# Seven quarter products for eight in the first channel product of blocks 1 to 3, and the second mixing layer in the order wr, wk, wv

## Chip, cores and metric

The kernel runs on one core of a Trainium2 chip. The metric is the device time of one execution in microseconds (us); of several executions the median is taken.

## What is computed

Three layers follow each other (reference, cut):

```python
x = attention(q, k, v, n_global, n_local)      # 2 x 8 heads x 768 x 64, joined to (2, 768, 512)
u = x + ((x.transpose(0, 2, 1) @ U) @ V).transpose(0, 2, 1)
x = u + np.maximum(u @ w_ch1, 0.0) @ w_ch2     # first channel layer: 512 -> 2048 -> 512
xk = mu_k * x + (1.0 - mu_k) * x_prev          # x_prev: x one token earlier, per batch
xr = mu_r * x + (1.0 - mu_r) * x_prev
k = np.maximum(xk @ w_k, 0.0)                  # 512 -> 1024
out = sigmoid(xr @ w_r) * (k * k @ w_v)        # 512 -> 512 and 1024 -> 512
```

Everything is float32. `x` has 1536 rows (2 batches of 768 tokens).

## The kernel before

The data lie with channels on the partitions (`yp`, four groups of 128 channels). The 1536 tokens are three chunks of 512: chunk 0 lies in the first batch, chunk 1 spans both (so its reads and writes of `yp` come in two pieces of 256), chunk 2 lies in the second. The first channel layer cuts its 2048 hidden channels into four blocks `g` of 512; block `g` needs the tiles `w1s` (its columns of `w_ch1`) and `w2s` (its rows of `w_ch2`).

Each matrix product is made of three passes (`PASS`): every operand is split into a high part and the remainder (low), and high*high, high*low and low*high are summed in PSUM. A product of 128 x 512 results over a depth of 512 is so 4 x 3 = 12 matmuls of 512 columns.

`m_ch1(g, c, f)` (L904) makes hidden tile `f` of block `g` and chunk `c`: 12 matmuls (L893) into a PSUM bank of tag `a`, ScalarE takes the relu as high part (L897), VectorE the low part (L901). `m_ch2(g, c, o)` (L909) makes 12 matmuls (L915) into a bank of tag `t` and VectorE adds them to `yp` (L919). There are four banks of each tag, so a matmul group waits until the group four before it on its tag has been read.

Weights arrive as 64-bit floats in pieces of 128 x 512 (512 KB), through three staging tiles `stg`. `bg` takes the next piece from the list `bgq`: VectorE and ScalarE turn it to float32 (`cvt` L655, L660, L664, L668), ScalarE writes the high part (L672), GpSimd the low part (L676). A staging tile is free for the next transfer when L668 has read it. Two slots each of the pools `sb`, `sc`, `sd` and three of `sa` hold weights, activations (`us`, the split input of a chunk; `rs`, a split hidden tile) and the mixed inputs.

`weave` interleaves lists of steps. The program on TensorE keeps the written order; on the other engines a scheduler orders the instructions at build time, so VectorE and ScalarE run each instruction in the order it set. The written order alternates first and second products:

```python
weave(st_ch1(1, 1, slot_b) + st_ch2(1, 0), st_bg(4))
weave(st_ch1(1, 2, slot_c) + st_ch2(1, 1), st_bg(4))
weave(st_ch1(2, 0, slot_b) + st_ch2(1, 2))
```

The second layer mixes each chunk with its shifted copy (`m_mix`, L1053 on GpSimd, L1055 on VectorE, split by L1057 and L1058), and then, per chunk, makes `k` (`m_k`: 96 matmuls L1071 in 8 tiles; relu, square and split by L1075 to L1081) and per tile of 128 tokens (`m_out`) the gate (12 matmuls L1090, sigmoid L1094) and the value (24 matmuls L1101), multiplied (L1104) and sent out (L1105).

## Time and profile before

| | |
|---|---|
| times of three runs | 518.87, 519.10, 520.76 us; median 519.1 |
| profiled execution | 521.29 us, of it a span of 519.4 us on the engines |
| TensorE matmuls | 504.9 us busy, 97% of the span |
| weight loads | 412.1 us, 79% |
| VectorE | 304.7 us, 59% |
| ScalarE | 217.7 us, 42% |
| GpSimd | 184.1 us, 35% |
| mean granted TensorE clock | 0.995 |

A matmul's busy time overlaps the next one's; the distance between two starts is the time it costs. Times in the rows count from the start of the span. Attention, the low-rank product and block 0 of chunk 0 fill the first 107 us; the rest is dense matmuls.

### The profile page before, as it was taken

The page shows a single profiled execution, that of the slowest core. Times are in us where ns is not written, and L with a number is a line of the kernel's source. Part 1 is how long each engine was busy: PE and PEld are TensorE (multiplying, and loading weights), DVE is VectorE, ACT ScalarE, POOL GpSimd, SP SyncE. Part 2 cuts the span into 40 slices and gives each one's busy share as a digit, 9 for nine tenths or more (in the row PEclk, how much of TensorE's full clock was granted, in tenths as well). Part 3 has the DMA queues.
Part 4 walks back from the last instruction along what each step waited for, and adds up shares of the span by engine and source line. Part 5 has one row for each costly group of instructions (what it writes and reads, how often), then busy time and mean ns, then how long its engine had stood idle before and what let it go on. Part 6 is the DMA issues. An engine that isn't in the chain of part 4 may idle for free.

```text
span 519.4 us, 8649 instructions
## 1 busy us (share of the span) xinstructions
PE 504.9 (97%) x3314; PEld 412.1 (79%) x3314; DVE 304.7 (59%) x672; ACT 217.7 (42%) x508; POOL 184.1 (35%) x247
## 2 busy tenths in 40 slices
PE   8899999989999999999999999999999999999995
PEld 4677688778888888888888888887888888888885
DVE  7899978989982826528265837796043522252110
ACT  6999986455521313214133312444912441144100
POOL 7767784034410404004040403636712442144100
PEclk9999999989999999999999999999999999999999
DMA  8988543313550311304113310031001000100001
GB/s 327 329 286 294 202 137 122 107 65 122 162 187 16 122 40 48 115 0 122 40 25 138 124 39 1 24 138 42 0 21 40 22 0 21 40 21 1 21 21 47
DMA packets 13586, 47.18 MB, mean 91 GB/s; under 512 B 1760, under 2 KB 2144, under 8 KB 13536
## 3 DMA queue, kind: packets, MB, share of 16 engines
...
## 4 chain that ended last, share of the span: by engine, by line
PE 81%; DVE 11%; DMA 2%; ACT 2%; issue 1%; POOL 1%; POOLq 0%; SPq 0%; DVEq 0%; ACTq 0%
PE aps L893 26%; PE bps L915 19%; PE pvs L1101 13%; PE kps L1071 11%; PE prs L1090 6%; DVE P L471 3%; PE tp L498 2%; DVE cvc L664 2%; DVE cvc L668 2%; PE s L463 2%; DMA stg<-in_w_dram 1%; PE warm L379 1%; DMA stg<-in_wv_dram 1%; DVE yp L919 1%; PE xa L513 1%
## 5 line engine op out<-in xcount | busy, mean ns | idle before, releaser
L893 PE MATMUL aps<-us,w1s 128*128 128x512 f32 x576 | 135.3, 393 | 0.0
L915 PE MATMUL bps<-rs,w2s 128*128 128x512 f32 x576 | 132.5, 389 | 0.0
L893 PEld LDWEIGHTS aps<-us,w1s 128*128 128x128 f32 x576 | 108.7, 189 | 22.7
L915 PEld LDWEIGHTS bps<-rs,w2s 128*128 128x128 f32 x576 | 108.0, 188 | 23.3 <-PE gps L792 0.8
L897 ACT ACTIVATE rs<-aps 128x512 fp32r<-128x512 f32 x48 | 28.4, 597 | 95.0 <-PE aps L893 94.7
L1071 PE MATMUL kps<-mix,wk 128*128 128x512 f32 x288 | 66.1, 389 | 0.4 <-ACT kf L1075 0.4
L1071 PEld LDWEIGHTS kps<-mix,wk 128*128 128x128 f32 x288 | 54.0, 188 | 12.0 <-ACT kf L1075 0.8
L1101 PE MATMUL pvs<-wv,kh 128*128 128x512 f32 (+1 forms) x208 | 61.9, 373 | 0.0
L901 DVE SCALAR_TENSOR_TENSOR rs<-aps,rs 128x512 fp32r<-128x512 f32 x48 | 32.7, 686 | 41.0 <-ACT rs L897 41.0
L664 DVE SCALAR_TENSOR_TENSOR cvc<-cvc,cvt 128x512 uint32<-128x512 uint32 (+1 forms) x53 | 48.6, 918 | 7.9 <-ACT cvc L660 6.4
L660 ACT ACTIVATE cvc<-stg 128x512 f32<-128x512 f32 (+1 forms) x53 | 35.2, 674 | 41.3 <-DMA stg<-in_w_dram 15.6
L919 DVE TENSOR_TENSOR yp<-bps,yp 128x512 f32<-128x512 f32 (+1 forms) x64 | 33.9, 550 | 25.5 <-PE bps L915 25.4
L491 POOL TENSOR_SCALAR P<-P,sm 128x192 f32<-128x192 f32 x96 | 42.1, 461 | 16.5 <-DVE sm L485 9.6
L1053 POOL TENSOR_SCALAR mixt<-yp,mu 128x512 f32<-128x512 f32 (+1 forms) x32 | 21.6, 682 | 74.1 <-DVE mixf L1055 29.6
L668 DVE SCALAR_TENSOR_TENSOR cvc<-stg,cvc 128x512 uint32<-128x512 uint32 x52 | 45.6, 885 | 0.7
L676 POOL TENSOR_TENSOR w2s<-cvc,w2s 128x512 fp32r<-128x512 f32 x16 | 23.2, 1467 | 63.5 <-ACT w2s L672 63.5
L1101 PEld LDWEIGHTS pvs<-wv,kh 128*128 128x128 f32 x208 | 38.1, 188 | 6.9
L676 POOL TENSOR_TENSOR w1s<-cvc,w1s 128x512 fp32r<-128x512 f32 x16 | 23.9, 1514 | 55.4 <-ACT w1s L672 54.8
L479 ACT ACTIVATE P<-P,nm 128x192 f32<-128x192 f32 x96 | 42.5, 447 | 1.5 <-DVE nm L471 1.4
L1081 POOL TENSOR_TENSOR kl<-kf,kh 128x512 fp32r<-128x512 f32 x24 | 31.0, 1293 | 30.6 <-ACT kh L1080 30.6
L1101 PE MATMUL pvs<-wv,kl 128*128 128x512 f32 (+1 forms) x104 | 38.8, 373 | 0.0
L1055 DVE SCALAR_TENSOR_TENSOR mixf<-yp,mu,mixt 128x512 f32<-128x512 f32 (+1 forms) x32 | 20.3, 653 | 29.8 <-POOL mixt L1053 29.7
...
## 6 DMA issues: line engine op xcount, KB each, us to landing
stg<-in_w_dram SPq DMA_DIRECT2D x32, 512.0 KB, 4.1
...
stg<-in_wk_dram SPq DMA_DIRECT2D x8, 512.0 KB, 4.2
stg<-in_wv_dram SPq DMA_DIRECT2D x8, 512.0 KB, 4.0
...
stg<-in_wr_dram SPq DMA_DIRECT2D x4, 512.0 KB, 3.6
```

The source lines that it names most:

```text
L479: nc.scalar.activation(out=Px, in_=Px, func=ACTF.Exp, scale=-1.0, bias=z["nm"][:, i, x:x + 1], accum_out=z["sm"][:, i, x:x + 1])
L491: engine.tensor_scalar(out=Px, in0=Px, scalar1=z["sm"][:, i, x:x + 1], scalar2=1.0, op0=ALU.mult, op1=ALU.mult)
L660: nc.scalar.activation(out=z["c"].bitcast(F32), in_=parts(z)[1].bitcast(F32), func=ACTF.Copy, scale=2.0 ** -112)
L664: nc.vector.scalar_tensor_tensor(out=z["c"], in0=z["c"], scalar=3, in1=z["t"], op0=ALU.logical_shift_left, op1=ALU.bitwise_or)
L668: nc.vector.scalar_tensor_tensor(out=z["c"] if plain is None else plain, in0=parts(z)[1], scalar=0x80000000, in1=z["c"], op0=ALU.bitwise_a ...
L676: engine.tensor_tensor(out=lo, in0=z["c"].bitcast(F32), in1=hi.bitcast(F32), op=ALU.subtract)
L893: nc.tensor.matmul(rs[g, c, f], lhsT=wsl(("w1", g), lw, kk, f * 128, 128), rhs=us[c][:, lx, kk, :], start=(kk == 0 and n == 0), stop=(kk = ...
L901: nc.vector.scalar_tensor_tensor(out=r[:, 1, f, :], in0=rs[g, c, f], scalar=0.0, in1=r[:, 0, f, :].bitcast(F32), op0=ALU.max, op1=ALU.subt ...
L915: nc.tensor.matmul(ps, lhsT=wsl(("w2", g), lw, f, o * 128, 128), rhs=r[:, lx, f, :], start=(n == 0), stop=(n == 11))
L919: nc.vector.tensor_tensor(out=ys, in0=ps[:, a:e], in1=ys, op=ALU.add)
L1071: nc.tensor.matmul(ps, lhsT=wsl("wk", lw, kk, f * 128, 128), rhs=xk[:, lx, kk, :], start=(n == 0), stop=(n == 11))
L1101: nc.tensor.matmul(pv, lhsT=ks[c][lx][:, f, t * 128:(t + 1) * 128], rhs=wsl("wv", lw, f, c0, c1 - c0), start=(n == 0), stop=(n == 23))
```

## The change

For blocks 1 to 3 the first products of chunks 1 and 2 are taken together (`st_pair`). With the block's weights A (hidden x input channels) and the inputs B (input channels x the two chunks) each cut into 2 x 2 quarters, the four quarters of A B need eight quarter products, each of 256 hidden channels, a depth of 256 and 512 tokens; Winograd's form needs seven:

- S1 = A21 + A22, S2 = S1 - A11, S3 = A11 - A21, S4 = A12 - S2, made by VectorE from the converted weights (tiles `raw`) and split into `w1x`;
- T1 = B12 - B11, T2 = B22 - T1, T3 = B22 - B12, and B21 - T2, made once, during block 0, by VectorE from `yp` and split into `diff` and, for T3, over a part of `us` of chunk 2 that is no longer needed after block 0;
- the products A11 B11, A12 B21, S4 B22, A22 (B21 - T2), S1 T1, S2 T2, S3 T3, six matmuls each for one of two tiles of hidden channels, added up by VectorE in tiles `sums` (seven additions L1023 and one ScalarE copy a tile), then relu (L1026) and low part (L1027) from there.

The order of the work becomes, for a block: the pair, then the first product of chunk 0, then the second products of chunks 2, 1 and 0; for block 3, which has no next block to load, chunks 0, 1 and 2. In the second layer the gates of a chunk (`m_r`) come ahead of its `m_k`, its weights are converted in the order wr, wk, wv; `sg` has six tiles of its own, VectorE makes every second low part of these weights, and the shifted product of `m_mix` moves from GpSimd to ScalarE.

```diff
+                        def add(_, z=z):
+                            a, b = z[0], z[1]
...
+                            nc.vector.tensor_tensor(out=s1, in0=a[:, 256:], in1=b[:, 256:], op=ALU.add)
+                            nc.vector.tensor_tensor(out=s3, in0=a[:, :256], in1=a[:, 256:], op=ALU.subtract)
+                            nc.vector.tensor_tensor(out=s2, in0=s1, in1=a[:, :256], op=ALU.subtract)
+                            nc.vector.tensor_tensor(out=s4, in0=b[:, :256], in1=s2, op=ALU.subtract)
...
+                            for i, t in enumerate(z["t"]):
...
+                                nc.scalar.copy(out=h, in_=t)
+                                nc.gpsimd.tensor_tensor(out=o, in0=t, in1=h.bitcast(F32), op=ALU.subtract)
...
+                    return [first, lambda: sub(t2, lo, t1), fourth, lambda: sub(z, lo, up)]
...
+                    def mm(n, j):
+                        a, b = OP[n]
+                        t = ps[n, j] = bank("at"[n in (1, 2, 3)], "pps")
+                        for k in range(2):
+                            for m, (lw, lx) in enumerate(PASS):
+                                nc.tensor.matmul(t, lhsT=a(lw, k, j), rhs=b(lx, k), start=(k == 0 and m == 0),
+                                                 stop=(k == 1 and m == 2))
...
+                        return [p1, p6, p2, p5, p3, p7, p4]
+
+                    return unit(0) + unit(1)
...
-                        nc.gpsimd.tensor_scalar(out=t[:, a:e], in0=yq, scalar1=mu[:, 2 + which, kk:kk + 1], scalar2=1.0,
-                                                op0=ALU.mult, op1=ALU.mult)
+                        nc.scalar.activation(out=t[:, a:e], in_=yq, func=ACTF.Copy, scale=mu[:, 2 + which, kk:kk + 1])
...
+                for g in range(1, NG):
+                    if g >= G0:
+                        weave(st_pair(g), st_bg(2))
...
+                    if g + 1 < NG:
+                        weave(st_ch1(g, 0, slot_b), st_bg(2))
+                        queue_pair(g + 1)
+                        weave(st_ch2(g, 2) + st_ch2(g, 1), st_bg(4))
+                        queue_g(g + 1, None, slot_c)
+                        weave(st_ch2(g, 0))
                 queue_weight("wr", wr, 4, 512, [slot_a("wr")])
...
+                queue_weight("wk", wk, 4, DK, [slot_d("wk0"), slot_d("wk1")])
+                weave(st_ch1(3, 0, slot_b), st_bg(4))
...
+                queue_weight("wv", wv, 8, 512, [slot_a("wv0"), slot_a("wv1")])
+                weave(st_ch2(3, 0), st_bg(3))
+                weave(st_ch2(3, 1), st_bg(2), st_mix(0, 1, slot_b))
+                weave(st_ch2(3, 2), st_bg(2), st_mix(0, 0, slot_b))
                 for c in range(NCH):
+                    weave([lambda t=t: m_r(c, t) for t in range(4)], st_bg(4))
```

**Place 1, TensorE, a block of the first layer.** `aps`, `pps` and `bps` are the PSUM banks of a first product, a quarter product and a second product; L915 is L948 and L893 is L926 in the changed kernel. Before:

```order
L893 MATMUL aps<-us,w1s 128x512 x48
L915 MATMUL bps<-rs,w2s 128x512 x48
L893 MATMUL aps<-us,w1s 128x512 x48
L915 MATMUL bps<-rs,w2s 128x512 x48
L893 MATMUL aps<-us,w1s 128x512 x48
L915 MATMUL bps<-rs,w2s 128x512 x48
L893 MATMUL aps<-us,w1s 128x512 x48
L915 MATMUL bps<-rs,w2s 128x512 x48
```

After, from the second half of block 1's pair on:

```order
L1019 MATMUL pps<-us,w1s 128x512 x6
L1019 MATMUL pps<-diff,w1x 128x512 x6
L1019 MATMUL pps<-us,w1s 128x512 x6
L1019 MATMUL pps<-diff,w1x 128x512 x6
L1019 MATMUL pps<-us,w1x 128x512 x12
L1019 MATMUL pps<-diff,w1s 128x512 x6
L926 MATMUL aps<-us,w1s 128x512 x48
L948 MATMUL bps<-rs,w2s 128x512 x144
L1019 MATMUL pps<-us,w1s 128x512 x6
```

Where groups of 48 alternated, the pair's groups of 6 (14 of them, 84 matmuls) stand ahead of chunk 0's 48, and all three second products (144) follow in one run.

**Place 2, VectorE, around the first hidden tiles of block 1 (before: those of chunk 0, after: those of the pair).** `cvt` is the first step of a weight conversion and waits for the transfer into its `stg`; `rs` is a low part; `sums` the additions of a pair. Before:

```order
L655 TENSOR_SCALAR cvt_2856<-stg_2854 128x512
L668 SCALAR_TENSOR_TENSOR cvc_2698<-stg_2694,cvc_2698 128x512
L901 SCALAR_TENSOR_TENSOR rs_2262<-aps_2263,rs_2262 128x512
L655 TENSOR_SCALAR cvt_2896<-stg_2894 128x512
L901 SCALAR_TENSOR_TENSOR rs_2262<-aps_2278,rs_2262 128x512
L901 SCALAR_TENSOR_TENSOR rs_2262<-aps_2303,rs_2262 128x512
L901 SCALAR_TENSOR_TENSOR rs_2262<-aps_2318,rs_2262 128x512
L919 TENSOR_TENSOR yp_63<-bps_2333,yp_63 128x512
L919 TENSOR_TENSOR yp_63<-bps_2347,yp_63 128x512
L919 TENSOR_TENSOR yp_63<-bps_2371,yp_63 128x512
```

After:

```order
L655 TENSOR_SCALAR cvt_2731<-stg_2729 128x512
L655 TENSOR_SCALAR cvt_2860<-stg_2858 128x512
L664 SCALAR_TENSOR_TENSOR cvc_2733<-cvc_2733,cvt_2731 128x512
L952 TENSOR_TENSOR yp_63<-bps_2338,yp_63 128x512
L668 SCALAR_TENSOR_TENSOR cvc_2733<-stg_2729,cvc_2733 128x512
L655 TENSOR_SCALAR cvt_2935<-stg_2933 128x512
L1023 TENSOR_TENSOR sums_2354<-pps_2363,sums_2354 128x512
L1023 TENSOR_TENSOR sums_2354<-pps_2371,sums_2354 128x512
L1023 TENSOR_TENSOR sums_2354<-pps_2381,sums_2354 128x512
L1027 SCALAR_TENSOR_TENSOR rs_2352<-sums_2354,rs_2352 128x512
L1023 TENSOR_TENSOR sums_2354<-pps_2399,sums_2354 128x512
L1023 TENSOR_TENSOR sums_2354<-pps_2409,sums_2354 128x512
```

The additions of the pair stand behind the last of the conversions of block 2's `w1s` and behind `cvt_2860` and `cvt_2935`, which wait for transfers.

**Place 3, VectorE, the first product of chunk 0 in block 3.** Its four low parts are `rs_3156` before and `rs_3446` after; `wk0` is a low part of wk. Before:

```order
L919 TENSOR_TENSOR yp_63<-bps_3141,yp_63 128x256 x2
L655 TENSOR_SCALAR cvt_3668<-stg_3666 128x512
L901 SCALAR_TENSOR_TENSOR rs_3156<-aps_3157,rs_3156 128x512
L901 SCALAR_TENSOR_TENSOR rs_3156<-aps_3172,rs_3156 128x512
L901 SCALAR_TENSOR_TENSOR rs_3156<-aps_3187,rs_3156 128x512
L901 SCALAR_TENSOR_TENSOR rs_3156<-aps_3202,rs_3156 128x512
L919 TENSOR_TENSOR yp_63<-bps_3217,yp_63 128x512
L664 SCALAR_TENSOR_TENSOR cvc_3639<-cvc_3639,cvt_3637 128x512
```

After, from behind the first of the four:

```order
L668 SCALAR_TENSOR_TENSOR cvc_3620<-stg_3616,cvc_3620 128x512
L934 SCALAR_TENSOR_TENSOR rs_3446<-aps_3472,rs_3446 128x512
L668 SCALAR_TENSOR_TENSOR cvc_3666<-stg_3662,cvc_3666 128x512
L655 TENSOR_SCALAR cvt_3716<-stg_3714 128x512
L664 SCALAR_TENSOR_TENSOR cvc_3718<-cvc_3718,cvt_3716 128x512
L676 TENSOR_TENSOR wk0_3444<-cvc_3666,wk0_3444 128x512
L934 SCALAR_TENSOR_TENSOR rs_3446<-aps_3497,rs_3446 128x512
L668 SCALAR_TENSOR_TENSOR cvc_3718<-stg_3714,cvc_3718 128x512
L655 TENSOR_SCALAR cvt_3768<-stg_3766 128x512
L664 SCALAR_TENSOR_TENSOR cvc_3770<-cvc_3770,cvt_3768 128x512
L655 TENSOR_SCALAR cvt_3818<-stg_3816 128x512
L934 SCALAR_TENSOR_TENSOR rs_3446<-aps_3522,rs_3446 128x512
```

The four low parts stood next to each other, and are now apart, with conversions of wk between them; two of these (`cvt_3768`, `cvt_3818`) wait for transfers ahead of the last low part.

## Rows read from the trace of the kernel before

**Rows 1.** page, parts 1 and 4: busy time by engine; the last chain by engine
```profile
PE 504.9 (97%) x3314; PEld 412.1 (79%) x3314; DVE 304.7 (59%) x672; ACT 217.7 (42%) x508; POOL 184.1 (35%) x247
...
PE 81%; DVE 11%; DMA 2%; ACT 2%; issue 1%; POOL 1%; POOLq 0%; SPq 0%; DVEq 0%; ACTq 0%
```

**Rows 2.** timeline, PE, blocks and second layer (start us, length us, then engine, line)
```profile
142.43 11.04 PE L893 MATMUL aps<-us,w1s 128*128 128x512 f32 x48
...
316.51 11.04 PE L893 MATMUL aps<-us,w1s 128*128 128x512 f32 x48
327.39 21.92 PE L915 MATMUL bps<-rs,w2s 128*128 128x512 f32 x96
349.15 11.04 PE L1071 MATMUL kps<-mix,wk 128*128 128x512 f32 x48
360.60 11.18 PE L1071 MATMUL kps<-mix,wk 128*128 128x512 f32 x48 [0.41 <-ACT kf L1075]
```

**Rows 3.** timeline, all engines, before the first matmuls of chunk 1
```profile
104.84 0.52 PE L823 MATMUL hps<-uv 96*128 96x256 f32 x3
105.60 0.43 DVE L655 TENSOR_SCALAR cvt<-stg 128x512 uint32<-128x512 uint32 x1 [1.60 <-DMA stg<-in_w_dram]
105.94 0.68 DVE L919 TENSOR_TENSOR yp<-bps,yp 128x512 f32<-128x512 f32 x1
...
106.68 1.16 PE L823 MATMUL hps<-uv 96*128 96x256 f32 x3 [1.32 <-DVE yp L919]
```

**Rows 4.** windows: busy us (count) of PE, PEld, DVE, ACT, POOL; clock; DMA
```profile
107.70:153.30 45.60, 45.60 (x195) 37.54 (x194) 41.75 (x64) 22.86 (x42) 18.51 (x12) 0.96 0.40 128
153.30:196.80 43.50, 43.50 (x193) 36.04 (x192) 21.30 (x33) 9.22 (x16) 5.96 (x4) 1.00 0.20 61
```

**Rows 5.** chain of waits, second layer (start us, us, engine, tile, line)
```profile
371.79 2.72 PE prs L1090 x12
374.51 5.44 PE pvs L1101 x24
```

**Rows 6.** groups by line and form: busy us, mean ns of one, idle before
```profile
L664 DVE SCALAR_TENSOR_TENSOR cvc<-cvc,cvt 128x512 uint32<-128x512 uint32 x52 | 47.9, 922 | 7.9 <-ACT cvc L660 6.4 <-DVE cvt L655 0.5
L668 DVE SCALAR_TENSOR_TENSOR cvc<-stg,cvc 128x512 uint32<-128x512 uint32 x52 | 45.6, 885 | 0.7
...
L901 DVE SCALAR_TENSOR_TENSOR rs<-aps,rs 128x512 fp32r<-128x512 f32 x48 | 32.7, 686 | 41.0 <-ACT rs L897 41.0
L1081 POOL TENSOR_TENSOR kl<-kf,kh 128x512 fp32r<-128x512 f32 x24 | 31.0, 1293 | 30.6 <-ACT kh L1080 30.6
...
L655 DVE TENSOR_SCALAR cvt<-stg 128x512 uint32<-128x512 uint32 x52 | 26.3, 507 | 8.5 <-DMA stg<-in_w_dram 4.5 <-DMA stg<-in_wk_dram 2.9 <-DMA stg<-in_wv_dram 0.8
...
L919 DVE TENSOR_TENSOR yp<-bps,yp 128x512 f32<-128x512 f32 x32 | 22.0, 686 | 21.3 <-PE bps L915 21.2
...
L1080 ACT CAST kh<-kf 128x512 fp32r<-128x512 f32 x24 | 14.9, 621 | 12.9 <-DVE kf L1079 12.6
...
L919 DVE TENSOR_TENSOR yp<-bps,yp 128x256 f32<-128x256 f32 x32 | 11.9, 414 | 4.2 <-PE bps L915 4.2
```

**Rows 7.** windows, PE: stretch, length, busy us (count), granted clock, DMA
```profile
13.00:19.00 6.00, 4.67 (x88) 1.00 0.97 322
108.00:112.00 4.00, 4.00 (x12) 0.57 0.00 0
```

**Rows 8.** timeline, PE, early attention
```profile
14.88 0.55 PE L498 MATMUL tp<-ident,P 128*128 128x128 f32 x3 [1.33 <-POOL P L491]
```

**Rows 9.** DMA issues: transfers of one weight piece, KB each, us to landing
```profile
stg<-in_wk_dram SPq DMA_DIRECT2D x8, 512.0 KB, 4.2
```

**Rows 10.** timeline, DVE, conversions of wk, beside POOL (next group) and alone
```profile
289.99 2.38 DVE L668 SCALAR_TENSOR_TENSOR cvc<-stg,cvc 128x512 uint32<-128x512 uint32 x2
...
294.13 0.69 DVE L668 SCALAR_TENSOR_TENSOR cvc<-stg,cvc 128x512 uint32<-128x512 uint32 x1
```

**Rows 11.** timeline, POOL, the same stretch
```profile
285.26 5.96 POOL L676 TENSOR_TENSOR wk<-cvc,wk 128x512 fp32r<-128x512 f32 x4 [15.77 <-ACT wk L672]
```

More of the change, by code (lines that the diff above doesn't have):

```diff
@@ L700, in queue_weight @@
                     wt[name] = (view, per)
-                    for kk in range(kt):
-                        for c0 in range(0, n, 512):
+                    for c0 in range(0, n, 512):
+                        for kk in range(kt):
                             hi = view[kk // per][:, 0, kk % per, c0:c0 + 512]
@@ L705, in queue_weight @@
                             s = src[kk * 128:(kk + 1) * 128, c0:c0 + 512]
-                            bgq.append((lambda d, s=s: nc.sync.dma_start(out=d, in_=s),
-                                        conv_steps((128, 512), hi, lo)))
+                            steps = conv_steps((128, 512), hi, lo)
+                            if name in ("wr", "wk", "wv") and kk % 2:
+                                steps[-1] = ("lo", lambda z, f=steps[-1][1]: f(z, "DVE"))
+                            bgq.append((lambda d, s=s: nc.sync.dma_start(out=d, in_=s), steps))
                 def wsl(name, l, kk, c0, n):
@@ L919, in m_ch2, with raw_tiles, diff_tiles @@
                         nc.vector.tensor_tensor(out=ys, in0=ps[:, a:e], in1=ys, op=ALU.add)
+                diffs, sums = [], {}
+                def raw_tiles():
+                    t = slots["sb"].tile([128, 4096], F32, tag="sb", name="sums")
+                    return [t[:, x * 512:(x + 1) * 512] for x in range(8)]
+                def diff_tiles():
+                    raws[:] = raw_tiles()
+                    diffs[:] = [diff_p.tile([128, 6144], F32R, name="diff").rearrange("p (l t k n) -> p l t k n", l=2, t=3, k=2)]
@@ new lines, in diff_raw, with sub, first, fourth @@
+                def diff_raw(k):
+                    d = diffs[0]
+                    (_, _, up), (_, _, lo) = chunk(yp, k, 2)[0], chunk(yp, k + 2, 2)[0]
+                    t1, t2, z, t4 = raws[4 * k:4 * k + 4]
+                    def sub(o, p, q):
+                        nc.vector.tensor_tensor(out=o, in0=p, in1=q, op=ALU.subtract)
+                    def first():
+                        for a, e, ys in chunk(yp, k, 1):
+                            sub(t1[:, a:e], up[:, a:e], ys)
+                    def fourth():
+                        for a, e, ys in chunk(yp, k + 2, 1):
+                            sub(t4[:, a:e], ys, t2[:, a:e])
+                    return [first, lambda: sub(t2, lo, t1), fourth, lambda: sub(z, lo, up)]
@@ new lines, in diff_split, with parts, diff_late @@
+                def diff_split(k):
+                    return [lambda x=x, t=t: parts(diffs[0], x, k, raws[4 * k + t]) for x, t in enumerate((0, 1, 3))]
+                raws = []
+                def parts(d, x, k, raw):
+                    h, o = d[:, 0, x, k, :], d[:, 1, x, k, :]
+                    nc.scalar.copy(out=h, in_=raw)
+                    nc.vector.tensor_tensor(out=o, in0=raw, in1=h.bitcast(F32), op=ALU.subtract)
+                def diff_late(k):
+                    h, o = us[2][:, 0, k, :], us[2][:, 1, k, :]
+                    nc.scalar.copy(out=h, in_=raws[4 * k + 2])
+                    nc.vector.tensor_tensor(out=o, in0=raws[4 * k + 2], in1=h.bitcast(F32), op=ALU.subtract)
@@ L1081, in m_k, with m_r @@
                     nc.gpsimd.tensor_tensor(out=kl[:, f, :], in0=kf, in1=kh[:, f, :].bitcast(F32), op=ALU.subtract)
[L1083 to L1084 removed]
+                gate = {}
+                def m_r(c, t):
                     xr = xs[c, 1]
@@ L1092, in m_out @@
                             n += 1
-                    sg = tmp_p.tile([128, 512], F32, tag="tmp", name="sg")
-                    nc.scalar.activation(out=sg, in_=pr, func=ACTF.Sigmoid)
+                    gate[c, t] = tmp_p.tile([128, 512], F32, tag="sg", name="sg", bufs=6)
+                    nc.scalar.activation(out=gate[c, t], in_=pr, func=ACTF.Sigmoid)
+                def m_out(c, t):
+                    b, i = divmod(c * 4 + t, NT)
+                    sg = gate[c, t]
                     last = (c, t) == (NCH - 1, 3)
```

112 lines of the change are left out of this document (88 added, 24 removed).

## The prediction

> **What bounds the kernel.** I read the page first: TensorE is busy for 97% of the span and makes 81% of the chain that ended last [rows 1]. Then the timeline of TensorE: from 142.43 to 316.51 sixteen groups of 48 matmuls follow each other, no row of them with an idle time in brackets. That is 174.08 / 16 = 10.88 us a group and 10.88 / 48 = 0.2267 us a matmul; 96 of L915 take twice that, 349.15 - 327.39 = 21.76 [rows 2]. After 107 us the time is therefore a count of matmuls times 0.2267, plus two idle times: 1.32 us at 106.68 [rows 3] and 0.41 at 360.60 [rows 2]. The next thing to look at is who could become late. VectorE is busy for 41.75 of the 45.6 us before block 1's second products end, and for only 21.30 of the 43.5 after them [rows 4]: the place of danger is where blocks 0 and 1 meet.
>
> **The change part by part.** The sum is made against the profiled execution, 521.29 us, and carried over to the median of the runs, 519.1, which lies 2.2 lower.
>
> *Matmuls.* A block's two chunks take 7 x 2 x 6 = 84 matmuls instead of 96 (place 1). Three blocks: 36 x 0.2267 = **-8.16**. A group of 6 opens a bank twice as often as one of 12. The chain has a group of 12 at 2.72 us and one of 24 at 5.44, both 0.2267 a matmul [rows 5], so a new bank costs nothing there; three groups of one matmul of 256 columns take 0.52 [rows 3], at most 0.06 each over half of 0.2267. The 54 more groups cost 0 to 3.2, and I take 0, by the nearer rows.
>
> *The idle time at 360.60* comes from ScalarE, which is late with k's relu because it still converts wv [rows 2]. In the change 48 gate matmuls, 10.88 us, stand ahead of the first k tile. **-0.41**; bounds -0.41 and 0.
>
> *The idle time at 106.68.* TensorE waits for VectorE's addition, and that stood behind a `cvt` which had waited 1.60 us for its transfer [rows 3]. In the changed order this `cvt` comes later; four half-width sums of weights stand ahead instead. The addition, at 105.94 before, comes at 105.94 - 1.60 - 0.4 + 4 x 0.41 = 105.6 by the half-width row [rows 6], 105.3 at half of the full width's 0.69. I take **-0.5**; bounds -1.3 (no wait) and +0.3.
>
> *The clock behind it.* In 108 to 112 TensorE is busy throughout at a granted 0.57, so most of it at the lower level, 1.2 GHz: 4 x 0.43 = 1.7 us lost [rows 7]. But an idle time of 1.33 us at 14.88 [rows 8] was followed by a clock of 1.00 [rows 7]. The trace does not tell which the shorter gap gets; I take 0, bounds -1.7 (no fall) and +1.7 (one more, behind a new gap). [...]
>
> *Additions of the pairs, VectorE.* Until the first of them, 12 full-width and 16 half-width differences and sums are added, 12 x 0.69 + 16 x 0.41 = 14.8 us, and four conversions move behind it, 4 x (0.92 + 0.89 + 0.51) = 9.3 [rows 6]. VectorE's 41.75 become 47.3 in 45.6 us [rows 4]: some 2 us late, and `cvt_2935` (place 2) can wait for a transfer. I put the first addition at 158, where its product ends at 153.3 + 2 x 1.36 = 156.0. TensorE does not wait for it: the bank is wanted again four groups of tag `a` later, at 153.3 + 8 x 1.36 = 164.2. In a pair VectorE has 11 instructions of 0.69, 7.5 us, for every 7 x 1.36 = 9.5 of TensorE, so it catches up; in blocks 2 and 3 it has 25 additions and low parts (17.3), 8 conversions (18.5), 8 half sums (3.3) and the additions to `yp` (8.8), 48 of 62.6 us. **0**; the upper bound is the first rival.
>
> *Chunk 0 of block 3* is the one place where a first product is followed by its own second product. The high part of its last tile is wanted 9 matmuls, 2.04 us, after that tile ends, the low part after 10, 2.27. In place 3 the last low part stands behind `cvt_3818`, whose transfer can only start when the second L668 has read its staging tile. The pair's last relu and low part hold the first two low parts and these L668 back to about 3.0 us before the tile ends; the transfer takes 4.2 [rows 9], landing at +1.2; behind it ScalarE makes a first step, a high part and the relu, 3 x 0.62 [rows 6], and VectorE the low part, 0.69: +3.0 or so against 2.27. **+0.8**; bounds 0 and 2.5 (0.8 with a fall of the clock behind it).
>
> *Between k and v* no gate lies any more. Of the last k tile relu, square, high and low part take 3 x 0.62 + 1.29 = 3.2 us [rows 6]; they are wanted 21 matmuls, 4.76, later. 0, with 1.6 to spare; two mixing steps on ScalarE in front, 4 x 0.62 = 2.5, would leave 0.9 a chunk, bound +2.7. The rest has cover: mixing steps on ScalarE lie beside at least 10.9 us of matmuls a chunk, `w1x` is split 22 us ahead of its use, and the last product, its multiplication and its transfer out are the same.
>
> Sum: -8.16 - 0.41 - 0.5 + 0.8 = -8.3. The profiled 521.29 becomes 513.0, the median **510.8**. The one case that this describes runs from 508.3 (no new wait, no fall of the clock) to 514.2 (a wait of 2.5 and a fall more).
>
> **Rivals.** *GpSimd holds VectorE up.* Two L668 took 2.38 us while GpSimd worked without a pause and 0.69 each alone [rows 10, 11], 0.5 more each. The added differences have both inputs in SBUF too, and lie among the same 12 GpSimd instructions, 18.5 us [rows 4]. I have counted about 7 of these as lost to VectorE in both kernels; if the other 11 are lost as well, the first addition comes at 169 and TensorE waits 5 us at 164.2: 515.8. For it speaks the full VectorE there; against it, that many additions read PSUM and L901 keeps its 0.69 [rows 6]. The Trainium skill, SBUF — State Buffer, in Who interferes with whom, says that an instruction with two SBUF inputs and one of GpSimd that reads SBUF shut each other out for a whole instruction; by that the sum would be 515.8, by the rows, where VectorE loses half of the time, 510.8.
>
> *A transfer decides block 3.* If one more transfer has to land ahead of the last low part, the wait at chunk 0's second product grows by 4.2 and the clock falls behind it, 1.7: 516.7, within half a per cent of before. For it: two `cvt` stand there. Against: three staging tiles, so both transfers run at once.
>
> *TensorE stops between quarter products: slower.* If VectorE is over 6 x 1.36 = 8.2 us late in the pairs, each product waits for a bank. One gap like that at 106.68 with the clock's fall costs 1.32 + 1.7 = 3.0; from four of them, 12, the gain of 8.3 is gone and the time is 522.8. It would need 8 us of lateness in blocks 2 and 3, where VectorE has 14 to spare. The Trainium skill, TensorE: Matmul & The Clock Gate, in the second failure mode, tells of a kernel whose cycling through PSUM banks left short idle times and a clock that swung; here groups of 12 ran at a clock of 1.00 [rows 4].
>
> That the change does not take out the matmuls can't be: the order shows 84.
>
> **How the numbers follow.** What a measurement of this kernel tells from no change is about 0.5%, 2.6 us. The forecast's case has 0.79; GpSimd 0.09 (515.8, still faster by 0.6%); the transfer 0.07 (same); stops between products 0.05 (slower). So faster 0.87, with one in a hundred of the first two falling short, same 0.08, slower 0.05. The range takes in the forecast's own, 508.3 to 514.2, and reaches to the GpSimd rival, 515.8; it leaves 0.12 out.
>
> **What would show it.** Right: in blocks 1 to 3 TensorE's rows of L1019 come in groups of 6 with 1.36 between their starts and no idle time, a block takes 62.6 us; no wait of L1221 on ScalarE; a wait of under 2 us ahead of the first L948 of block 3; the clock at 1.00 behind block 0. Wrong: idle times of L1019 released by VectorE L1023 (first or third rival), a wait of 4 us or more at block 3's L948 (second), a clock below 1.00 in a pair, a matmul pace above 0.2267 in groups of 6, or waits of L1256 on GpSimd's low part.

## Result and profile after

| | before | after |
|---|---|---|
| median of four runs each, same chip | 519.16 us (518.87 to 520.76) | 512.95 us (512.60 to 515.65) |
| ratio of the times | | 0.9885, 95% interval 0.9846 to 0.9925 |
| profiled execution, its span | 521.29, 519.4 us | 512.60, 510.8 us |
| mean granted TensorE clock | 0.995 | 0.997 |

The forecast was 510.8 us, in a range of 508.3 to 515.8: the time lies in the range and the sign is as forecast; the gain is 6.2 us instead of 8.3. The page of the changed kernel, as in [rows 1]: busy time of TensorE, its weight loads, VectorE, ScalarE and GpSimd, and the last chain by engine.

```profile
PE 496.1 (97%) x3278; PEld 404.0 (79%) x3278; DVE 357.5 (70%) x768; ACT 249.9 (49%) x566; POOL 167.9 (33%) x217
...
PE 84%; DVE 10%; DMA 2%; issue 1%; ACT 1%; POOL 1%; POOLq 0%; SPq 0%; DVEq 0%
```

VectorE has risen from 304.7 to 357.5 us and TensorE fallen from 504.9 to 496.1; TensorE still makes the chain. Its timeline from the end of block 0 on, in the columns of [rows 2]:

```profile
105.12 0.52 PE L856 MATMUL hps<-uv 96*128 96x256 f32 x3
106.28 1.16 PE L856 MATMUL hps<-uv 96*128 96x256 f32 x3 [0.65 <-DVE yp L952]
107.28 0.39 PE L926 MATMUL aps<-us,w1s 128*128 128x512 f32 x1
...
129.55 21.92 PE L948 MATMUL bps<-rs,w2s 128*128 128x512 f32 x96
151.31 1.52 PE L1019 MATMUL pps<-us,w1s 128*128 128x512 f32 x6
152.67 1.52 PE L1019 MATMUL pps<-diff,w1x 128*128 128x512 f32 x6
...
170.35 11.04 PE L926 MATMUL aps<-us,w1s 128*128 128x512 f32 x48
...
213.87 1.52 PE L1019 MATMUL pps<-us,w1s 128*128 128x512 f32 x6
...
306.35 2.20 PE L948 MATMUL bps<-rs,w2s 128*128 128x512 f32 x9
309.20 0.50 PE L948 MATMUL bps<-rs,w2s 128*128 128x512 f32 x1 [0.64 <-ACT rs L930]
311.20 30.71 PE L948 MATMUL bps<-rs,w2s 128*128 128x512 f32 x134 [1.50 <-DVE rs L934]
341.75 11.04 PE L1241 MATMUL prs<-wr,mix 128*128 128x512 f32 x48
352.62 21.92 PE L1221 MATMUL kps<-mix,wk 128*128 128x512 f32 x96
```

The second row answers to [rows 3]: 1.32 us of idle time have become 0.65. The pair of block 1 begins at 151.31, each group of six starts 1.36 after the one before, and the pair ends at 170.35, 19.04 later: 84 matmuls of 0.2267. From pair to pair lie 62.56 us. Nothing is in brackets until 309.20: there TensorE waits 0.64 for ScalarE's relu (L930) and at 311.20 another 1.50 for VectorE's low part (L934), at the second product of chunk 0 in block 3. Idle times are counted between modelled ends; by the distance between starts, 306.35 to 341.75 is 35.40 us for 144 matmuls, which make 32.64 at 0.2267 each, so that the two waits cost 2.76 and not 2.14. Behind them, gates and k tiles follow each other without a wait; the 0.41 of [rows 2] is gone.

The same 98 matmuls at the end of block 0 stand between these two rows of the kernel before, and between 107.28 and 129.55 after:

```profile
107.68 0.40 PE L893 MATMUL aps<-us,w1s 128*128 128x512 f32 x1
...
131.55 11.04 PE L915 MATMUL bps<-rs,w2s 128*128 128x512 f32 x48
```

That is 23.87 us against 22.27: the fall of the clock of [rows 7], which is missing after, cost 1.60. So by the starts in the two profiled executions: -8.16 for the matmuls, -0.57 at 360.60 (the second 48 began 11.45 behind the first instead of 10.88), -0.68 at 106 (1.84 from the first three matmuls to the next before, 1.16 after), +2.76 in block 3 and -1.60 for the clock. That is -8.25; the two executions differ by 521.29 - 512.60 = 8.7, and 0.4 is not located.

The fall of the clock differs between executions of the same kernel, which matters for the medians. In the windows of the kernel before, run once more on another chip, and of the changed kernel, also run once more (stretch, length, busy us and count of TensorE, weight loads, VectorE, ScalarE, GpSimd; granted clock; DMA):

```profile
108.00:112.00 4.00, 4.00 (x13) 3.07 (x13) 4.00 (x11) 1.79 (x6) 0.00 (x0) 0.66 0.03 12
```

```profile
108.00:112.00 4.00, 4.00 (x19) 3.28 (x18) 4.00 (x10) 2.65 (x7) 1.19 (x1) 1.00 0.25 98
312.00:316.00 4.00, 4.00 (x11) 3.19 (x12) 3.97 (x6) 2.52 (x4) 1.49 (x1) 0.58 0.50 168
```

Before, TensorE stops for 1.43 us at 107.42 (1.32 in [rows 3]) and the clock is at 0.66 behind it, so partly at its lower level of 1.2 GHz. After, the stop of 0.66 us is followed by a clock of 1.00, and the two stops of block 3 by 0.58.

### The profile page after: what moved, and what is told of

Same layout as the page of the kernel before. It is cut to its first block, busy times and chain, and to the rows that moved or that the text cites. A ratio compares the mean times of both kernels' runs of the same rounds, so it can differ in the third digit from the quotient of the medians.

```text
span 510.8 us, 8694 instructions
## 1 busy us (share of the span) xinstructions
PE 496.1 (97%) x3278; PEld 404.0 (79%) x3278; DVE 357.5 (70%) x768; ACT 249.9 (49%) x566; POOL 167.9 (33%) x217
## 4 chain that ended last, share of the span: by engine, by line
PE 84%; DVE 10%; DMA 2%; issue 1%; ACT 1%; POOL 1%; POOLq 0%; SPq 0%; DVEq 0%
PE bps L948 23%; PE pvs L1256 13%; PE kps L1221 13%; PE pps L1019 11%; PE aps L926 11%; PE prs L1241 6%; DVE P L471 3%; PE tp L498 2%; PE s L463 2%; DVE cvc L664 1%; DMA stg<-in_wk_dram 1%; PE warm L379 1%; DVE cvc L668 1%; DMA stg<-in_w_dram 1%; PE xa L513 1%
## 5 line engine op out<-in xcount | busy, mean ns | idle before, releaser
L948 PE MATMUL bps<-rs,w2s 128*128 128x512 f32 x576 | 132.2, 390 | 2.1 <-DVE rs L934 1.5
L948 PEld LDWEIGHTS bps<-rs,w2s 128*128 128x128 f32 x576 | 108.0, 188 | 26.1 <-DVE rs L934 1.8
L926 PE MATMUL aps<-us,w1s 128*128 128x512 f32 x288 | 67.6, 391 | 0.0
L926 PEld LDWEIGHTS aps<-us,w1s 128*128 128x128 f32 x288 | 53.7, 188 | 11.0
L1256 PE MATMUL pvs<-wv,kh 128*128 128x512 f32 (+1 forms) x208 | 60.4, 373 | 0.0
L664 DVE SCALAR_TENSOR_TENSOR cvc<-cvc,cvt 128x512 uint32<-128x512 uint32 (+1 forms) x53 | 46.9, 894 | 1.9 <-ACT cvc L660 1.2
L1256 PEld LDWEIGHTS pvs<-wv,kh 128*128 128x128 f32 x208 | 38.1, 188 | 6.9
L1229 DVE SCALAR_TENSOR_TENSOR kf<-kps,kf 128x512 f32<-128x512 f32 x16 | 11.0, 688 | 46.0 <-ACT kf L1225 46.0
L1256 PE MATMUL pvs<-wv,kl 128*128 128x512 f32 (+1 forms) x104 | 38.8, 373 | 0.0
L668 DVE SCALAR_TENSOR_TENSOR cvc<-stg,cvc 128x512 uint32<-128x512 uint32 x52 | 37.6, 732 | 0.4
L1023 DVE TENSOR_TENSOR sums<-pps,sums 128x512 f32<-128x512 f32 x42 | 28.7, 688 | 12.0 <-PE pps L1019 11.3
L655 DVE TENSOR_SCALAR cvt<-stg 128x512 uint32<-128x512 uint32 (+1 forms) x53 | 30.4, 576 | 7.3 <-DMA stg<-in_w_dram 5.7
L1259 DVE TENSOR_TENSOR sg<-pvs,sg 128x512 f32<-128x512 f32 (+1 forms) x13 | 8.4, 647 | 35.6 <-PE pvs L1256 35.6
L1241 PE MATMUL prs<-wr,mix 128*128 128x512 f32 x144 | 33.1, 389 | 0.0
```

What stands on the lines that cost most here:

```text
L664: nc.vector.scalar_tensor_tensor(out=z["c"], in0=z["c"], scalar=3, in1=z["t"], op0=ALU.logical_shift_left, op1=ALU.bitwise_or)
L668: nc.vector.scalar_tensor_tensor(out=z["c"] if plain is None else plain, in0=parts(z)[1], scalar=0x80000000, in1=z["c"], op0=ALU.bitwise_a ...
L926: nc.tensor.matmul(rs[g, c, f], lhsT=wsl(("w1", g), lw, kk, f * 128, 128), rhs=us[c][:, lx, kk, :], start=(kk == 0 and n == 0), stop=(kk = ...
L948: nc.tensor.matmul(ps, lhsT=wsl(("w2", g), lw, f, o * 128, 128), rhs=r[:, lx, f, :], start=(n == 0), stop=(n == 11))
L1241: nc.tensor.matmul(pr, lhsT=xr[:, lx, kk, t * 128:(t + 1) * 128], rhs=wsl("wr", lw, kk, 0, 512), start=(n == 0), stop=(n == 11))
L1256: nc.tensor.matmul(pv, lhsT=ks[c][lx][:, f, t * 128:(t + 1) * 128], rhs=wsl("wv", lw, f, c0, c1 - c0), start=(n == 0), stop=(n == 23))
```

## Experiments

The times come from three chips: the first four kernels below ran on one; the changed kernel once more, both placings of the low parts and the late additions on a second; the others on a third, each time with the kernel before beside them. Ratios are to the kernel before on the same chip.

**The kernel before, once more.** No edit.

> The kernel before once more, for a second trace of it. Theory: the profiled execution of 521.29 us held a fall of TensorE's clock (granted 0.57 in 108 to 112 us) that most executions do not have, so that its distance of 2.2 us to the median is that fall. Then this execution, if it is one of the common ones, has a span of about 517.5 us, a mean clock of 0.998, a granted clock of 1.00 in 108 to 112 and the same idle time of 1.3 us at 106.7. Rival: the fall belongs to the idle time of 1.32 us and comes every time; then span 519.4 and 0.57 again, and the 2.2 us lie outside the span or elsewhere.

Measured: 521.27 us median of ten; ratio 0.9999 [0.9975, 1.0024]. The profiled execution took 521.88, with the idle time of 1.43 and the fall shown above. Of the ten, the four with a mean clock of 0.998 or 0.999 took 519.5 to 520.2, the six with 0.995 or 0.996 took 521.0 to 523.4. Of the executions of the kernel before beside the experiments, 10 of 16, 6 of 23 and 5 of 15 on the three chips had a clock of 0.996 or less. A mean clock of 0.996 or less is taken here as the sign of the fall; the window itself was profiled in two executions of this kernel, and both held it. By that sign the fall is neither always there nor a rarity, so that theory and rival were each half right; it is worth 1.60 us by the starts above, and the two groups of the ten lie about 2 us apart. The profile on which the prediction rested held it; three of the four times that make the median of 519.16 in the result, at 518.87 to 519.22, look by their length as if they had not (520.76 as if it had).

**Block 3's second products in the order 1, 0, 2.**

```diff
-                weave(st_ch2(3, 0), st_bg(3))
-                weave(st_ch2(3, 1), st_bg(2), st_mix(0, 1, slot_b))
-                weave(st_ch2(3, 2), st_bg(2), st_mix(0, 0, slot_b))
+                weave(st_ch2(3, 1), st_bg(3))
+                weave(st_ch2(3, 0), st_bg(2))
+                weave(st_ch2(3, 2), st_bg(2), st_mix(0, 1, slot_b) + st_mix(0, 0, slot_b))
```

> Block 3's second products in the order chunk 1, 0, 2 instead of 0, 1, 2, both mixing steps of chunk 0 beside chunk 2's. Theory: the 0.64 + 1.50 us that TensorE waits for chunk 0's last relu and low part in block 3 go, since they have 10.9 us more; nothing else gets late: 512.95 - 2.1 = 510.8, span 508.7. Rival: the conversions of wk set the pace of the stretch and the wait comes back ahead of the first gate or k tile: 512.5 to 513. Third: the mixing steps of chunk 0, now beside one product instead of two, come late for the first gate: a wait of L1241 on mix, slower than 513.

Measured: 510.29 us (510.0 to 510.98), ratio 0.9798 [0.9775, 0.982]. TensorE's timeline:

```profile
306.60 32.80 PE L948 MATMUL bps<-rs,w2s 128*128 128x512 f32 x144
...
358.82 13.89 PE L1221 MATMUL kps<-mix,wk 128*128 128x512 f32 x60 [0.37 <-ACT sg L1245]
```

The three products of block 3 run through in 32.6 us. One new wait of 0.37 stands in the first k tiles, behind a sigmoid; that is all that is left of the rival. The first theory holds.

**Conversions of wk behind the last relu and low part.** (`fen` keeps these two instructions; `issue_after` orders what is traced in it behind them, on their engines.)

```diff
-                weave(st_ch1(3, 0, slot_b), st_bg(4))
+                weave(st_ch1(3, 0, slot_b), st_bg(6))
...
-                weave(st_ch2(3, 0), st_bg(3))
+                with tc.issue_after(fen["r"].ins), tc.issue_after(fen["l"].ins):
+                    bg(3)
+                weave(st_ch2(3, 0))
```

> Order of the products as in the change, but the conversions of wk are put behind the last relu (ScalarE) and the last low part (VectorE) of chunk 0 in block 3. Theory (the conversions that stand ahead of these two make the wait): the wait is gone, 512.95 - 2.1 = 510.8; wk is converted some 5 us later, of which nothing is seen, since its first k tile is wanted 45 us after. Rival (the additions of the pair or the product itself make it late): a wait of 1 us or more stays at the same place. Second rival: wk is then late for its first k tile, L1221 waits for it, 512 or more.

Measured: 513.68 us (512.98 to 514.28), ratio 0.986 [0.9837, 0.9884]. The wait in block 3 is gone, and TensorE's timeline has these instead:

```profile
368.27 5.75 PE L1222 MATMUL kps<-mix,wk 128*128 128x512 f32 x24 [1.54 <-ACT kf L1226]
...
379.19 0.50 PE L1257 MATMUL pvs<-wv,kh 128*128 128x512 f32 x1 [0.22 <-ACT kh L1231]
380.54 0.50 PE L1257 MATMUL pvs<-wv,kl 128*128 128x512 f32 x1 [0.85 <-POOL kl L1232]
```

(Lines are one higher in this kernel.) These are 2.61 us of idle time where 2.14 were removed, and the 510.8 of the theory is missed. It is not wk that comes late, as the second rival had it, but wv: between 353 and 367 ScalarE makes nine instructions for wv, where the changed kernel has four from 353 to 381, and is late with the relu of a k tile. The wait in block 3 does hang on the conversions ahead of it; this place for them is no better. The edit also takes six pieces for four beside chunk 0's first product, and no run separates the two.

**Without the pairs.** Twelve-matmul products for all chunks, no differences, no sums of weights (`G0` = 4).

> The change without the quarter products (12-matmul products for chunks 1 and 2 in all blocks, no differences, no sums of weights), with its order of products and its second layer. Theory: three pairs are worth 36 x 0.2267 = 8.16 us and little else: 512.95 + 8.16 = 521.1 less what of the wait in block 3 (2.1) and of the idle time at 106.3 (0.65) belongs to the pairs: 519 to 521.1. Rival: the pairs lose part of their gain to VectorE's load or to the bank changes: under 518.5.

Measured: 523.58 us (521.37 to 525.54), ratio 1.0052 [1.002, 1.0084], above what I expected. The wait in block 3 is 2.38 us here, and the clock in 320 to 324 is 0.59 behind it. The rest of the change, with its low parts on GpSimd, is therefore no gain by itself: without the pairs it is 0.5% slower.

**The changed kernel, once more.** No edit.

> The changed kernel once more, beside the others of this call. Theory: its idle time of 0.65 us at 106.3 brings no fall of the clock, the wait of 2.1 us in block 3 does in some executions: two groups of times, about 2.9 us apart (the four times so far: 512.6, 512.8, 513.1 at a clock of 0.997, and 515.65 at 0.993), against the kernel before 6 to 8 us less. Rival: the 515.65 was a chance of that execution; all times lie within 1 us.

Measured: 514.51 us median of six, ratio 0.9893 [0.9875, 0.9911]. One execution took 512.66 at a clock of 0.997; five took 514.28 to 515.15 at 0.993 or 0.994. The profiled one (514.98) has the same waits as before, 0.65 and 1.51, and the fall at 312 to 316 shown above. From the start of block 3's second products to the first gate matmul pass 36.96 us (307.06 to 344.02), 4.32 more than 144 matmuls take, where the execution without a fall lost 2.76. So the wait costs 2.76 us and the fall behind it about 1.6: by the mean clock in five of six executions here, and in one of four of the result (515.65, clock 0.993). The theory's two groups are there, 1.6 to 2.5 us apart instead of 2.9.

**Low parts of wr, wk and wv all on GpSimd; all on VectorE.** The change gives every second one to VectorE.

```diff
-                            if name in ("wr", "wk", "wv") and kk % 2:
+                            if False:
```

> The changed kernel with every low part of wr, wk and wv on GpSimd again (ten instructions moved back from VectorE). First theory: the wait in block 3 comes from the conversions that stand ahead of the last relu and low part; VectorE is relieved of two or three instructions of 0.7 to 0.9 us there, so that the wait stays or shrinks by up to 1 us, and the time is within 0.7 us of the changed kernel's. Rival (GpSimd's work beside VectorE stretches VectorE's instructions, the cvt of 1.35 us beside a GpSimd low part where 0.42 is usual): more such instructions, a wait of 3 us or more and 1 to 3 us slower.

```diff
-                            if name in ("wr", "wk", "wv") and kk % 2:
+                            if name in ("wr", "wk", "wv"):
```

> The changed kernel with every low part of wr, wk and wv on VectorE, none on GpSimd. Rival theory (GpSimd stretches VectorE): the cvt in front of the last low part of block 3 takes 0.42 instead of 1.35, the wait of 1.50 on that low part shrinks by about 0.9: 0.9 faster. First theory (the order of conversions): two more instructions of 0.69 stand in the stretch, the wait is the same or up to 1.4 longer: equal or slower by up to 1.4.

Measured: all on GpSimd 518.58 us (517.64 to 518.93), ratio 0.9975 [0.9964, 0.9985]; all on VectorE 510.29 us (509.87 to 510.46), ratio 0.9816 [0.9798, 0.9834]; the change beside them 514.51. More work on VectorE made the kernel 4.2 us faster and less made it 4.1 us slower. Both signs are those of the GpSimd theory, and both sizes are above what was expected of it, 0.9 and 1 to 3: the falls of the clock come and go with the waits. All on GpSimd, TensorE stops four times, 4.23 us in all:

```profile
307.74 1.07 PE L948 MATMUL bps<-rs,w2s 128*128 128x512 f32 x3 [0.27 <-DVE rs L934]
310.07 0.73 PE L948 MATMUL bps<-rs,w2s 128*128 128x512 f32 x2 [1.26 <-DVE rs L934]
312.30 0.80 PE L948 MATMUL bps<-rs,w2s 128*128 128x512 f32 x1 [1.49 <-ACT rs L930]
314.30 6.02 PE L948 MATMUL bps<-rs,w2s 128*128 128x512 f32 x16 [1.21 <-DVE rs L934]
```

All on VectorE it doesn't stop in block 3 at all. Why is seen in the changed kernel between 303 and 312, all engines:

```profile
303.56 1.62 POOL L676 TENSOR_TENSOR wk<-cvc,wk 128x512 fp32r<-128x512 f32 x1 [5.09 <-ACT wk L672]
303.95 1.52 DVE L655 TENSOR_SCALAR cvt<-stg 128x512 uint32<-128x512 uint32 x1
...
306.62 0.68 ACT L660 ACTIVATE cvc<-stg 128x512 f32<-128x512 f32 x1 [1.44 <-DMA stg<-in_wk_dram]
...
307.31 0.68 DVE L668 SCALAR_TENSOR_TENSOR cvc<-stg,cvc 128x512 uint32<-128x512 uint32 x1
307.91 0.42 DVE L655 TENSOR_SCALAR cvt<-stg 128x512 uint32<-128x512 uint32 x1
308.03 0.62 ACT L672 CAST wk<-cvc 128x512 fp32r<-128x512 f32 x1 [0.73 <-DVE cvc L668]
...
308.55 0.59 ACT L930 ACTIVATE rs<-aps 128x512 fp32r<-128x512 f32 x1
308.72 1.53 POOL L676 TENSOR_TENSOR wk<-cvc,wk 128x512 fp32r<-128x512 f32 x1 [3.54 <-ACT wk L672]
309.19 1.35 DVE L655 TENSOR_SCALAR cvt<-stg 128x512 uint32<-128x512 uint32 x1
...
310.46 0.68 DVE L934 SCALAR_TENSOR_TENSOR rs<-aps,rs 128x512 fp32r<-128x512 f32 x1
...
311.20 3.06 PE L948 MATMUL bps<-rs,w2s 128*128 128x512 f32 x12 [1.50 <-DVE rs L934]
```

and, for a `cvt` without GpSimd beside it, in the kernel with all low parts on VectorE:

```profile
303.31 0.42 DVE L655 TENSOR_SCALAR cvt<-stg 128x512 uint32<-128x512 uint32 x1
...
306.12 7.06 PE L948 MATMUL bps<-rs,w2s 128*128 128x512 f32 x29
...
307.08 0.59 ACT L930 ACTIVATE rs<-aps 128x512 fp32r<-128x512 f32 x1
...
308.04 0.68 DVE L934 SCALAR_TENSOR_TENSOR rs<-aps,rs 128x512 fp32r<-128x512 f32 x1
```

A `cvt` takes 0.42 us (307.91), and 1.52 and 1.35 where a GpSimd low part had already begun. It then ends 0.29 us after GpSimd's instruction does: 303.56 + 1.62 = 305.18 against 303.95 + 1.52 = 305.47, and 308.72 + 1.53 = 310.25 against 310.54. So it did not run slower beside GpSimd; it waited for its end. In the whole trace of the changed kernel from 100 us on, 50 VectorE instructions that read nothing from PSUM begin while GpSimd is in a subtraction of 128x512; 46 of them end 0.28 to 0.29 us (the `cvt` and half-width ones) or 0.54 to 0.56 us behind GpSimd's end. The other four begin where GpSimd itself takes 2.27 or 3.16 us. The 29 that read an operand from PSUM keep their 0.41 or 0.68 to 0.69. The two `cvt` cost 1.10 + 0.93 = 2.03 us. The first holds up the L668 (307.31) behind which ScalarE's L672 (308.03) and with it the relu (308.55) stand, the second stands ahead of the last low part (310.46). With 2.03 taken off the 2.76, an estimate, 0.7 us would be left for the conversions that stand ahead of the last low part by the order alone. The transfer at which I had looked, that of the second `cvt`, kept nobody waiting; the one before it landed by 306.62 and kept ScalarE waiting 1.44, VectorE not at all. The Trainium skill, SBUF — State Buffer, in Who interferes with whom, says that whichever of VectorE and GpSimd issues first holds the shared ports for the whole instruction and the other is blocked, for VectorE instructions with two inputs in SBUF and for those in its two-port modes; the rows agree, with the 0.29 and 0.55 behind GpSimd's end as the measured sign. The `cvt` has one input, and that it takes 0.42 where two-input instructions of its size take 0.68 is the only sign here that it runs in such a mode.

**GpSimd's work beside VectorE, without moving any.** The kernel with all low parts on VectorE, and for every second piece the same subtraction also on GpSimd into a tile that nothing reads (this adds work, and leaves the result as it is).

```diff
+                        if eng == "both":
+                            idle_t = (tmp_p.tile([128, 512], F32R, tag="idle", name="idle", bufs=1) if tmp_p else
+                                      raw_p.tile([128, 512], F32R, tag="raw", name="idle"))
+                            nc.gpsimd.tensor_tensor(out=idle_t, in0=z["c"].bitcast(F32), in1=hi.bitcast(F32), op=ALU.subtract)
...
+                                steps[-1] = ("lo", lambda z, f=steps[-1][1], odd=kk % 2: f(z, "DVE" if odd else "both"))
```

> The kernel with all low parts of wr, wk, wv on VectorE (low_dve), and ten needless GpSimd subtractions of the same operands beside them, into tiles that nothing reads: the order of VectorE's instructions is that of low_dve, GpSimd has the load of the changed kernel. Theory: it is GpSimd's work beside VectorE that makes the last low part of chunk 0 in block 3 late; then instructions of 1.2 to 1.8 us instead of 0.42 to 0.69 stand there again and TensorE waits 1.5 us or more at the same place: 512 to 515. Rival: it was the order on VectorE and ScalarE; then no wait and 510.3.

Measured: 512.70 us (512.38 to 513.02), ratio 0.985 [0.9825, 0.9876]. From all engines' timeline in block 3 (lines four higher; L678 is the needless subtraction):

```profile
304.44 1.90 POOL L678 TENSOR_TENSOR idle<-cvc,wk 128x512 fp32r<-128x512 f32 x1 [6.16 <-ACT wk L672]
...
305.71 1.18 DVE L668 SCALAR_TENSOR_TENSOR cvc<-stg,cvc 128x512 uint32<-128x512 uint32 x1
...
309.00 0.73 PE L952 MATMUL bps<-rs,w2s 128*128 128x512 f32 x2 [0.63 <-ACT rs L934]
...
310.06 3.23 PE L952 MATMUL bps<-rs,w2s 128*128 128x512 f32 x13 [0.33 <-DVE rs L938]
310.20 1.56 POOL L678 TENSOR_TENSOR idle<-cvc,wk 128x512 fp32r<-128x512 f32 x1 [3.86 <-ACT wk L672]
310.52 1.79 DVE L680 TENSOR_TENSOR wk<-cvc,wk 128x512 fp32r<-128x512 f32 x1
```

The time lies in the range of the theory. VectorE's and ScalarE's instructions have the same order in the two traces from 95 us on, so that GpSimd's work is all that differs. TensorE waits again, 0.63 + 0.33 = 0.96 us, less than the 1.5 that the theory wanted; by the starts the 144 matmuls from 306.17 on take 1.5 us longer than without a wait. L668 (0.68 elsewhere) takes 1.18 and ends 0.55 after GpSimd (306.89 against 306.34), L680, the low part, 1.79 (312.31 against 311.76). Here these blocked instructions stand in other places than the `cvt` of the change. GpSimd alone is thus shown to bring back 0.96 of 2.14 us of idle time, or 1.5 of 2.76 by the starts; that the rest hangs on which instruction meets GpSimd, and so on the order, is argued from the rows above and not shown by a run of its own. (A further 0.86 at 379.02, on a low part of k on GpSimd, adds to this kernel's time.)

**Late additions in the pair.** Ten needless copies on VectorE ahead of block 1's first addition; the result stays.

```diff
                         def p6():
                             mm(6, j)
+                            if g == 1 and j == 0:
+                                for _ in range(10):
+                                    nc.vector.tensor_copy(out=w1, in_=ps[6, j])
```

> The changed kernel with ten needless VectorE copies (128x512 out of PSUM, 0.6 us from start to start) ahead of the first addition of block 1's pair, to find the point from which late additions stop TensorE. That addition ended at 158.86 and the bank is wanted again by the first product but one of the second half, at 162.19: 3.3 us of slack. Theory: 6.0 us of delay give an idle time of 2.7 us at that product (L1019, released by VectorE L1023) and little after it, 2.7 slower, or 4.5 to 5.5 with a fall of the clock behind the gap. Rival: the slack is larger (or the order on VectorE gives way) and nothing is lost; or each later product waits too, and the loss is 6 or more.

Measured: 520.17 us (517.83 to 521.44), ratio 1.0001 [0.9981, 1.0022], beside 514.51 for the change: 5.7 us lost. TensorE and VectorE around the place, and TensorE's clock:

```profile
160.92 1.98 PE L1019 MATMUL pps<-us,w1s 128*128 128x512 f32 x8
166.01 2.70 PE L1019 MATMUL pps<-diff,w1x 128*128 128x512 f32 x6 [3.12 <-DVE sums L1023]
...
175.43 11.04 PE L926 MATMUL aps<-us,w1s 128*128 128x512 f32 x48
```

```profile
157.95 7.21 DVE L1041 COPY sums<-pps 128x512 f32<-128x512 f32 x10
165.26 2.08 DVE L1023 TENSOR_TENSOR sums<-pps,sums 128x512 f32<-128x512 f32 x3
```

```profile
166.00:170.00 4.00, 3.99 (x11) 3.13 (x12) 3.84 (x7) 1.26 (x2) 0.00 (x0) 0.57 0.00 0
```

The copies took 7.2 us instead of 6.0, and the product that waits is the one that was named, the second of the second half (166.01, 3.73 later than its group's turn, 162.28). No other product of the pair waits, but the clock is at 0.57 for 4 us. From 160.92 to the pair's end (175.43) pass 14.51 us where the change takes 170.35 - 160.83 = 9.52: 5.0 lost in the place itself, of the 5.7; the expectation had 4.5 to 5.5 with a fall. In block 3 TensorE waits 0.65 + 1.84 here, 0.3 more than in the change. So the slack of 3.3 us was real, and in this trace a gap in a pair cost its length and a fall.

**The pairs and the new second layer, each priced without the wait.** The kernel with all low parts on VectorE, without the pairs (as above); and with the pairs, but wk, wr, wv and gates inside `m_out` as before.

```diff
-                    weave([lambda t=t: m_r(c, t) for t in range(4)], st_bg(4))
-                    weave([lambda f=f: m_k(c, f) for f in range(8)], st_bg(8),
-                          st_mix(c + 1, 1, slot_b) if 0 < c < NCH - 1 else [])
...
+                    weave([lambda f=f: m_k(c, f) for f in range(8)], st_bg(8))
+                    weave([lambda t=t: (m_r(c, t), m_out(c, t)) for t in range(4)],
+                          st_mix(c + 1, 0, slot_b) if c + 1 < NCH else [])
```

> low_dve without the quarter products, to price the pairs without the wait in block 3 and the falls of the clock that follow it. Theory: 36 matmuls at 0.2267 are all that the pairs are worth, and some 0.5 to 0.6 for the idle time at 106 (1.19 without the differences and sums, 0.63 with them): 510.3 + 8.2 + 0.6 = 519.0, 1.7 more where the clock falls behind that idle time. Rival: quarter products cost TensorE something more (their 54 more groups): under 518.3.

> low_dve with the second layer in the old order (wk, wr, wv; k tiles first, the gate of a tile of tokens ahead of its value), to price the new order. Theory: the new order is worth the idle time of 0.41 us of ScalarE behind the conversions of wv, so 510.3 + 0.4 = 510.7, with a wait of that size ahead of a k tile of chunk 0. Rival: with six of the eight last conversions now later than in the kernel before, k tiles wait more than once: 512 or more. Other rival: no wait, 510.3, and the order is worth nothing.

Measured: without the pairs 520.01 us (519.68 to 521.47), ratio 0.9987 [0.9971, 1.0003]; pairs and old second layer 510.10 (509.62 to 512.06), ratio 0.9795 [0.9769, 0.9821]. The first has these waits:

```profile
106.56 1.16 PE L856 MATMUL hps<-uv 96*128 96x256 f32 x3 [1.24 <-DVE yp L952]
...
319.89 30.67 PE L948 MATMUL bps<-rs,w2s 128*128 128x512 f32 x134 [0.53 <-DVE rs L934]
```

Against the kernel with the pairs that is 1.24 - 0.67 = 0.57 at 106 and in block 3 0.53, or 0.82 by the starts (316.94 to 350.40 for 144 matmuls), so that of the difference of 9.9 us 8.16 + 0.57 + 0.82 = 9.55 are accounted for, and 0.4 are not located. Nothing speaks for a hidden cost of the quarter products. With the old second layer no wait stands ahead of any k tile either, and the time is that of the new one: once GpSimd is out of the way, the order wr, wk, wv is worth nothing that was measured.

**Both remedies.** Order 1, 0, 2 and all low parts of wr, wk, wv on VectorE.

> Both remedies together: second products of block 3 in the order 1, 0, 2 and all low parts of wr, wk, wv on VectorE. Each alone gave 510.29 on its chip. Theory: they take out the same wait, so the sum is no better than one, 510.0 to 510.5, without the 0.37 us that the first k tiles waited for a gate in the order 1, 0, 2 if that came from conversions; rival: VectorE, now with both mixing steps beside one product and ten more low parts, is late for the first gates or k tiles: 511 or more.

Measured: 510.10 us (509.61 to 510.73), ratio 0.9801 [0.9778, 0.9824]. The only wait behind the attention is the one at 106.50, 0.68 us. The two remedies take out the same wait. Either of them takes 1.8 to 2.0% less than the kernel before, the change 1.1%.

## Why the prediction was right, and where it was off

- *Matmuls, -8.16*: right. 19.04 us a pair, groups of six at 1.36, banks cost nothing.
- *Idle time at 360.60, -0.41*: gone, as predicted; by the starts it was worth 0.57. It also goes without the new order.
- *Idle time at 106.68, -0.5*: -0.68, for the reason given: the addition came at 105.55, predicted 105.3 to 105.6.
- *The clock behind it, 0*: wrong, and with it the way from the profiled execution to the median. By the mean clock, the stop of 1.3 to 1.4 us is followed by the fall in a quarter to two thirds of the executions; the one of 0.65 is followed by none in any profile. The change removes the fall (near the low bound of -1.7: -1.60); but the median of before had no fall to lose, so that "the median lies 2.2 lower" was true of before only. After, the profiled execution, 512.60, lies 0.35 below its median.
- *Additions of the pairs, 0*: right. The first one was put at 158:

```profile
158.17 2.08 DVE L1023 TENSOR_TENSOR sums<-pps,sums 128x512 f32<-128x512 f32 x3
```

- *Chunk 0 of block 3, +0.8*: the place and the waiting instructions were right, the size was not: 2.14 of idle time, within the bound of 2.5, but 2.76 by the starts, above it; the sign named for a right forecast, a wait of under 2 us, was missed by either count. I had the last low part stand behind a `cvt` that waits for its transfer. It stood behind a `cvt` that waited for GpSimd, and the relu behind another. The 0.8 was also added up wrongly: 1.2 + 3 x 0.62 + 0.69 is 3.75 and not 3.0, so that the same terms give 1.5.
- *Between k and v, 0*: right, no wait of L1256.
- *Slips that decide nothing*: a block has 14 groups for 8, so that there are 18 more groups and not 54, and their bound is 1.1 and not 3.2; the additions and low parts of a block are 26 and not 25; and what ends at 153.30 in [rows 4] is block 1's first product of chunk 0.

Put together: 513.0 was forecast for the profiled execution and 512.60 measured, and that nearness is luck: 1.96 more of the wait stand against 1.60 of the clock. For the medians, where there was no fall to lose, 8.16 + 0.57 + 0.68 - 2.76 = 6.65 us of gain stand against 6.2 measured; the remaining 0.45 is not located. That the median came out 2.15 above its forecast is thus for the most part (1.96) the wait of block 3, which was sized without GpSimd and added up too low.

Of the rivals, *GpSimd holds VectorE up* had the right mechanism in the wrong place: in the pair of block 1, GpSimd has nothing to do between 151 and 170, and in block 3, which I had not priced so, it decided. The rows 10 had been read as VectorE losing half of the time; an instruction that reads nothing from PSUM loses what is left of GpSimd's, and the additions that read PSUM lose nothing, as the prediction argued against this rival. *A transfer decides block 3*: no transfer was waited for by VectorE there. *TensorE stops between quarter products*: did not happen; the ten copies show one such stop costing what was said, its length and a fall. The slack was smaller than the text had it, 3.3 us for the first addition (162.19, the start of the second half's second product, less 158.86) instead of 164.2 - 158.7 = 5.5, since the pair began 2 us earlier than forecast and the addition did not.
